# A gated mix of attention and a Mish layer: first scores by halves of the tokens, head group 0 first, Mish in six 16-bit instructions, and a newly planned order

## The chip, the cores and the metric

The kernel runs on one core of a Trainium2 chip. The core's engines take their own instructions in their own order and wait for each other by semaphores: TensorE (PE, matmuls into PSUM; its weight loads are listed as PEld), VectorE (DVE), ScalarE (ACT), GpSimd (POOL) and SyncE (SP, which here only starts transfers). The metric is the device time of one execution in microseconds, the median of several runs.

## The reference

For 2048 tokens x of 640 numbers in bfloat16, two layers are computed and mixed by a gate of each token:

```python
x = A_x
g = _sigmoid((x * gate_w).sum(-1, keepdims=True))
a = _A_ref(x, A_wqkv, A_wo)       # attention: 32 heads of 20, all 2048 keys, softmax, @ wo
b = _B_ref(x, B_w1, B_b1, B_w2)   # h = x @ w1 + b1 (1536 wide); h * tanh(softplus(h)); @ w2
return g * a + (1 - g) * b
```

The attention's scale is 20 ** -0.5. The largest part is 32 heads x 2048 x 2048 scores, each with an exponential.

## The kernel before, in words

**Tiling.** The tokens are cut into four chunks of 512 (index c, as queries), the heads into eight groups of four (index g). A group's four heads lie in rows 32 apart, 20 rows used and 12 zero, so that four score matmuls of 32 rows run side by side in the array. For a pair (c, g) there are 16 key tiles of 128 (kt) and four heads (j): 64 *units*, each one bank of 128 keys x 512 queries; 2048 units in all. The last pair is split into two halves of 256 queries (`CUTS`).

**A unit's way.** PE computes its scores (line 1206, from QT and KT). Then one of two engines takes the exponential. ScalarE takes two or three units in one instruction (line 1233, "ETS", a pair of 1024 elements or a triple of 1536 per partition) out of one of two sets of three PSUM banks. Or VectorE takes a unit alone ("block", line 1291): it turns the scaled score into an integer whose bits are a 16-bit float near the exponential; when a tile's four heads are done, two shading passes (line 1321, 128x2048 int16) make two shifted copies, and the three are weighed with copies of V that GpSimd scales (line 1346, "VS"). PE multiplies all with V (line 1442) into one accumulator bank (ACC); V has a column of ones in front, so a row of the result is the softmax's sum.

**A pair's end.** VectorE copies the accumulator (line 1533, "OUNG"); three transfers on SP's queue and a reciprocal spread the inverted sums (RR, SUMS, BCT), and GpSimd multiplies (line 1499) into QT, which now holds the attention's output. For the last halves VectorE does this alone (lines 1518 to 1526).

**The start.** SP loads the first 512 tokens as rows in two halves (slots `xr0`, `xr1`), then the other chunks by transposing loads (`xt1`, `xt2`), three loads of the remaining query, key and value weights, and the last chunk (`xt3`). ScalarE loads its table and then issues group 0's weights (`wq0`, `wk0`, `wv0`). PE turns the rows by matmuls with a unit matrix (line 787); the query and key weights of group 0 are copied by GpSimd into zeroed areas with 32 columns a head (PADQ, PADK, line 599) and projected (lines 796 and 775). Keys and queries of the other groups are projected in rows of 128 or 120, written to memory and fetched back in the padded layout. PE fills waits with matmuls that nothing reads (line 1732; ten ahead of the start, line 576).

**The other layer.** h is computed for 256 tokens at a time (`h_task`, 48 evictions, line 984), and for two evictions at once Mish (`mish`): ScalarE takes tanh (line 1008), VectorE three instructions of 1024 float32 elements (lines 1025 to 1027). There are 24 Mish. The second product (`b_task`), the output product of the attention (`p_task`, `part_task`) and the mix with the gate (line 1064) follow; the last chunk's come at the very end.

**What sets the order.** The whole program is laid out on the host by a planner, and each engine executes its list as it stands. `Plan.add` keeps a clock for each engine with fixed costs (`EXP_PAIR`, `WIDE`, `BROAD`, `TAIL`). Per step one ScalarE exponential is placed; ahead of it come the scores of two steps later, with a third unit or a block for VectorE as the rules allow; between them PE gets the value products and the tasks (projections and the other layer), sorted by due times in steps; VectorE's queue of small work (`blend` for Mish, `soon` for shading) is filled into the gaps that the planner sees. The thresholds of these rules are constants which the table `STRETCHES` replaces from given steps on:

```python
if fast and step in STRETCHES:
    globals().update({**USUAL, **STRETCHES[step]})
```

The pairs' sequence is `groups`: for each g the chunks 0 and 1, and after all g the chunks 2 and 3 with all their groups. A second program for scores beyond a bound stands behind a flag and does not run.

Of the kernel before, what the change touches and what calls it, by code (L numbers as in the profile page):

```python
# [17 lines left out]
P = 128  # L18
S = 2048
D = 640  # L20
# [74 lines left out]
BROAD = 1.13  # L95
# [13 lines left out]
CALM = 10  # L109
# [5 lines left out]
H_AT = 160  # L115
H_STEP = 13.632
# [17 lines left out]
    11: {"BUSY": 0.327, "LATER": 0.616, "LOAD": 0.63, "MARGIN": 1.659, "OVER": 0.315, "PATIENCE": 7.796, "VMIN": 2.077},  # L134
    33: {"BEHIND": 29.477, "BUSY": 0.327, "FREE": 0.045, "KEPT": 12, "LATER": 0.616, "LOAD": 0.63, "MARGIN": 1.659, "NEED": 3, "OVER": 0.315, "PATIENCE": 7.796, "VMIN": 2.077},
    55: {"AHEAD": 49, "BEHIND": 29.477, "BUSY": 0.516, "CROWD": 1.326, "EAGER": 161, "FMIN": 0.057, "FREE": 0.045, "KEPT": 11, "LATER": 0.616, "LOAD": 0.63, "MARGIN": 1.659, "NEED": 3, "OVER": 0.284, "PATIENCE": 7.796, "ROOM": 2.074, "SLACK": 0.21, "THIRD": 0.53, "VMIN": 2.077, "XSLACK": 0.452},
    77: {"AHEAD": 49, "BEHIND": 29.477, "BUSY": 0.516, "CALLED": 8.459, "CROWD": 1.326, "EAGER": 161, "FMIN": 0.057, "FREE": 0.045, "KEPT": 12, "LATER": 0.616, "LOAD": 0.63, "MARGIN": 1.659, "NEED": 3, "OVER": 0.284, "PATIENCE": 13.174, "ROOM": 2.074, "SLACK": 0.21, "THIRD": 0.53, "VMIN": 2.077, "XSLACK": 0.452},
    97: {"MARGIN": -0.33, "ROOM": 1.622, "VMIN": 1.002},
    119: {"BUSY": 1.408, "EAGER": 125, "FREE": 0.15, "LOAD": 0.572, "MARGIN": -0.33, "NEED": 2, "OVER": 0.193, "ROOM": 1.622, "VMIN": 1.002},
    141: {"LATER": 0.556, "LOAD": 0.574, "MARGIN": 2.071, "OVER": 0.124, "SPUN": 0.577, "STREAM": 0.516, "XLATE": 6.941},  # L140
    163: {"AHEAD": 29, "CROWD": 1.874, "EAGER": 48, "FMIN": 0.467, "MARGIN": 0.792, "PATIENCE": 6.502, "SLACK": 0.282, "VMIN": 0.963},
    185: {"FREE": 0.148, "MARGIN": 1.463, "THIRD": 0.244, "XSLACK": 0.494},
    206: {"AHEAD": 45, "KEPT": 6, "THIRD": 0.693},
    227: {"BUSY": 0.518, "MARGIN": 1.193, "SPARED": 2},
# [142 lines left out]
def bass_gated_mix__softmax_full_mha__dense_activation_mish__prompt_kernel(  # L287
# [123 lines left out]
    def attention(pl, fast):  # L411
# [1580 lines left out]
```

## Time and profile before

| | |
|---|---|
| runs, us | 763.28, 759.77, 760.76; median 760.76 |
| the profiled execution | 761.41 us; its span from first to last instruction 759.6 us |
| busy: PE, DVE, ACT, POOL | 731.4, 697.2, 737.7, 200.3 us |
| granted TensorE clock | 0.998 |
| ScalarE exponentials | 703 pairs, 46 triples |
| VectorE blocks, shading passes | 504, 252 |
| first exponential starts, last ends | 10.15, 750.94 us |

An engine's busy time is the union of its instructions, and the mean duration of one overlaps the next a little, so the price of one in a dense row is better read from a stretch. Idle time in square brackets stands ahead of a row, with what ended it.

### The profile page before, as it was taken

What the parts mean: (1) busy time and instruction counts of PE and PEld (TensorE: products, weight loads), DVE (VectorE), ACT (ScalarE), POOL (GpSimd) and SP (SyncE); (2) the same over time, 40 slices, a digit from 0 to 9 for tenths busy, and PEclk for the clock granted to TensorE, in tenths of its full rate; (3) what the DMA queues carried; (4) which work ended last, traced back from release to release, by engine and by line L of the source; (5) the groups of instructions that cost most, each with busy time, mean ns of one, the idle gap of its engine ahead of it and who ended that gap; (6) DMA issues with size and microseconds to landing.
All of it is one profiled execution on the core that took longest, in us unless ns stands there. A gap on an engine that the chain in (4) does not pass through costs nothing.

```text
span 759.6 us, 25333 instructions
## 1 busy us (share of the span) xinstructions
PE 731.4 (96%) x11227; PEld 275.0 (36%) x11232; DVE 697.2 (92%) x1124; ACT 737.7 (97%) x780; POOL 200.3 (26%) x305
## 2 busy tenths in 40 slices
PE   8999999999999999889999999999999999998996
PEld 3333344334333433223333334333443433342343
DVE  3599878999999999997899999999999999999896
ACT  5999999999999999999999999999999999999995
POOL 3212233203223311342121333112442032322222
PEclk9999999999999999999999999999999999999999
DMA  9422421122134122361232122201212211300001
GB/s 222 75 67 50 120 66 35 59 66 58 50 105 116 47 81 68 98 177 43 53 61 67 37 68 68 78 11 54 84 51 63 83 29 38 90 26 16 16 7 51
DMA packets 78012, 50.41 MB, mean 66 GB/s; under 512 B 21408, under 2 KB 73880, under 8 KB 77848
## 3 DMA queue, kind: packets, MB, share of 16 engines
q1 hardware_dynamic: 75528, 48.24, 23.5%
q8 instruction: 90, 1.47, 0.8%
q10 hardware_dynamic: 2256, 0.47, 0.3%
q0 software_dynamic: 112, 0.01, 0.2%
q14 instruction: 26, 0.21, 0.1%
HBM read 39.01 MB, written 8.90 MB: 63 GB/s over the span
## 4 chain that ended last, share of the span: by engine, by line
PE 37%; ACT 32%; DVE 23%; DMA 4%; SPq 1%; issue 1%; POOL 1%; ACTq 0%; DVEq 0%
ACT ETS L1233 31%; PE PS L1206 12%; PE PS L507 12%; PE PS L1442 10%; DVE LN L1291 7%; DVE LN L1321 5%; DVE REG L1291 2%; PE PS L850 2%; DMA XB<-in_A_x_dram 2%; DMA BCT<-SUMS 1%; DVE U L1026 1%; SPq L556 1%; DVE HB L1027 1%; ACT REG L1008 1%; DVE HB L984 1%
## 5 line engine op out<-in xcount | busy, mean ns | idle before, releaser
L1233 ACT ACTIVATE ETS<-PS 128x1024 bf16<-128x1024 f32 (+1 forms) x749 | 716.0, 1117 | 7.1 <-PE PS L1206 6.0
L1206 PE MATMUL PS<-QT,KT 32*128 32x512 bf16 (+1 forms) x2120 | 293.5, 378 | 11.0 <-ACT ETS L1233 9.1
L1291 DVE TENSOR_SCALAR LN<-PS 128x512 int16<-128x512 f32 x400 | 266.5, 680 | 16.8 <-PE PS L1206 15.5
L1499 POOL TENSOR_TENSOR QT<-OUNG,BCT 128x512 bf16<-128x512 f32 x31 | 43.7, 1411 | 471.6 <-DMA BCT<-SUMS 471.6
L1346 POOL TENSOR_SCALAR VS<-V_all 128x84 bf16<-128x84 bf16 x260 | 149.1, 574 | 65.9 <-DVE V_all L831 26.3
L1206 PEld LDWEIGHTS PS<-QT,KT 32*128 32x128 bf16 x2120 | 73.0, 91 | 237.5 <-ACT ETS L1233 198.0
L1442 PE MATMUL PS<-ETS,V_all 128*21 128x512 bf16 (+1 forms) x1592 | 148.4, 376 | 0.4 <-DVE V_all L831 0.3
L1321 DVE TENSOR_SCALAR LN<-LN 128x2048 int16<-128x2048 int16 x178 | 126.7, 714 | 5.7 <-PE PS L1442 5.4
L507 PE MATMUL PS<-XB,REG 128*32 128x256 bf16 (+2 forms) x1860 | 95.8, 299 | 1.5 <-DMA XB<-in_A_x_dram 0.8
L1442 PE MATMUL PS<-LN,VS 128*21 128x512 f16 (+1 forms) x804 | 76.5, 379 | 2.9 <-DVE LN L1321 2.8
L507 PE MATMUL PS<-W2R,HB 128*32 128x320 bf16 x1536 | 75.4, 301 | 0.6 <-DVE LN L1291 0.4
L1442 PEld LDWEIGHTS PS<-ETS,V_all 128*21 128x21 bf16 x1592 | 37.9, 90 | 56.2 <-issue 45.7
L507 PEld LDWEIGHTS PS<-XB,REG 128*32 128x32 bf16 x1860 | 42.4, 95 | 30.7 <-issue 20.7
L507 PE MATMUL PS<-WOQ,QT 128*32 128x320 bf16 x1024 | 50.5, 301 | 0.5 <-DVE QT L1526 0.5
L507 PEld LDWEIGHTS PS<-W2R,HB 128*32 128x32 bf16 x1536 | 34.6, 96 | 26.9 <-issue 14.0
L1291 DVE TENSOR_SCALAR REG<-PS 128x512 int16<-128x512 f32 x56 | 37.1, 679 | 3.3 <-PE PS L1206 3.3
L1442 PE MATMUL PS<-LN,V_all 128*21 128x512 f16 (+1 forms) x408 | 39.0, 377 | 0.0
L507 PE MATMUL PS<-XB,WOQ 128*32 128x512 bf16 (+2 forms) x440 | 35.1, 382 | 0.8 <-DVE WOQ L739 0.4
L1442 PEld LDWEIGHTS PS<-LN,VS 128*21 128x21 bf16 x804 | 19.1, 89 | 42.3 <-issue 21.5
L984 DVE TENSOR_TENSOR HB<-PS,B1F 128x512 bf16<-128x512 f32 x48 | 32.5, 677 | 0.1
L507 PEld LDWEIGHTS PS<-WOQ,QT 128*32 128x32 bf16 x1024 | 23.4, 96 | 17.2 <-issue 8.0
L850 PE MATMUL PS<-REG,XB 128*128 128x160 bf16 (+1 forms) x240 | 24.5, 234 | 0.4 <-DVE V_all L860 0.2
(118 smaller groups left out, 502.1 us busy)
## 6 DMA issues: line engine op xcount, KB each, us to landing
REG<-in_B_w_dram SPq DMA_DIRECT2D x36, 320.0 KB, 3.3
BCT<-SUMS SPq DMA_DIRECT2D x31, 256.0 KB
W2R<-in_B_w_dram SPq DMA_DIRECT2D x12, 320.0 KB, 5.6
QT<-QS SPq DMA_DIRECT2D x28, 128.0 KB, 2.8
KT<-KS SPq DMA_DIRECT2D x28, 128.0 KB
KS<-LN SPq DMA_DIRECT2D x16, 128.0 KB, 4.0
QS<-WOQ SPq DMA_DIRECT2D x16, 120.0 KB
W2R<-in_B_w_dram SPq DMA_DIRECT2D x12, 160.0 KB, 5.2
```

The source lines that it names most:

```text
L507: last = e.matmul(to[at + j:at + j + n, :], w[:, j:j + n], x, start=start, stop=stop, tile_position=(0, at + j))
L556: "sp", lambda e: e.dma_start_transpose(xt(c), x_ap[c * CW:(c + 1) * CW, :]), (), f"xt{c}", cost=4.5)]
L850: return lambda e, bank: e.matmul(PS[:, bank, i * n:(i + 1) * n], xt(t // 4)[:, f, t % 4 * P:(t % 4 + 1) * P], WV[:, f, g * HD:g * HD + n] ...
L984: ev = dve(lambda e: e.tensor_tensor(hb, PS[:, bank, :].rearrange("p (i t) -> p i t", i=2), bias, ALU.add), [last, *b1f, *guarded, *b_read ...
L1008: ex = pl.add("act", lambda e: e.activation(U, h, AF.Tanh, bias=BEND, scale=0.5), [ev, u_free[0]], cost=0.94)
L1206: op = pl.add("pe", lambda e, to=to, g=real(g), tile=tile, j=j, cols=cols, c=c, of_q=of_q: e.matmul(to[:, cols], KT[32 * j:32 * j + 32, g, ...
L1233: e_op[s] = pl.add("act", lambda e: e.activation(RING[:, p:p + n, :], scores(s)[:, 0:n, :], AF.Exp, scale=SCALE), [s_op[s], *(pv_slot[b] f ...
L1291: bank_free[bank] = x_ops[bank] = tile["op"] = dve(lambda e: e.tensor_scalar(dst, PS[:, bank, :], SCALE * ULPS, BASE, ALU.mult, ALU.add), ...
L1321: op = pl.add("dve", lambda e: e.tensor_scalar(to, src, SHADES[n] - SHADES[held], None, ALU.add), [made, *deps], cost=SHADE, port=True)
L1346: weighted[(c, g, k)] = n, [pl.add("pool", lambda e, i=i, n=n, src=src: e.tensor_scalar(VS[:, n, i, :, :], src, WEIGHTS[i + 1], None, ALU. ...
L1442: lasts[n] = pl.add("pe", lambda e, v=v, j=j, src=src[:, cols], of_q=of_q, begin=begin, end=end: e.matmul(PS[32 * j:32 * j + EW, ACC, of_q ...
L1499: oung_free[0] = bc_read[0] = otn_done[(c, g)] = pl.add("pool", lambda e: e.tensor_tensor(otn(c, g), src, BC, ALU.mult), deps, cost=TIMES, ...
```

## The change

The first scores: the ten transposes of the first 256 tokens, their queries and their keys come ahead of all work on the second 256. Queries (chunk 0) and keys (all chunks) of group 0 are projected straight from the loaded weights, 20 columns a head, by the new `heads`; PADK is gone, PADQ stays for the other chunks' queries. The scores of the first two key tiles are cut into halves of the queries. ScalarE issues group 0's weight loads ahead of its table load; six matmuls, not ten, stand ahead of the start; the accumulator's fill moves behind the first keys.

The order: `groups` starts with group 0 of all four chunks, then groups 1 to 7 of chunks 0 and 1 in turn, then chunk 2, then chunk 3. Some planner costs and due times are new (loads' tails, `K_AT`, `V_AT`, `CALM` 10 to 6), and the whole `STRETCHES` table is.

Mish: the same polynomial of tanh, factored, on two halves of U2 seen as float16, with a factor `LIFT` that the gate's constant takes out again. U is free after the first of the six.

```diff
-BROAD = 1.13
+FULL = 0.60
+SCALED = 0.34
+LIFT = 512.0
...
-    11: {"BUSY": 0.327, "LATER": 0.616, "LOAD": 0.63, "MARGIN": 1.659, "OVER": 0.315, "PATIENCE": 7.796, "VMIN": 2.077},
...
+    119: {},
+    141: {"LOAD": 0.475, "OVER": 0.255},
...
-            groups = [(c, g) for g in range(NG) for c in range(2)] + [(c, g) for c in range(2, NC) for g in range(NG)]
+            groups = [(c, 0) for c in range(NC)]
+            groups += [(c, g) for cs in ((0, 1), (2,), (3,)) for g in range(1, NG) for c in cs]
...
+            if fast and (c, g) == (0, 0) and kt < 2:
+                return [(i, slice(i * HW, (i + 1) * HW), slice(kt * HW, (kt + 1) * HW)) for i in range(2)]
...
+            wload("wq0", WQ[:, :, 0:HD], wqkv[:, :, 0:HD], 4.4)
+            wload("wk0", WK[:, :, 0:HD], wqkv[:, :, D:D + HD], 4.4)
+            wload("wv0", WV[:, :, 0:HD], wqkv[:, :, 2 * D:2 * D + HD], 7.3)
             pl.add("act", lambda e: e.activation(U2[:, 0:1], RING[:, 0, 0:1], AF.Exp), [m_zero], cost=1.5)
-            wload("wq0", WQ[:, :, 0:HD], wqkv[:, :, 0:HD])
-            wload("wk0", WK[:, :, 0:HD], wqkv[:, :, D:D + HD])
-            wload("wv0", WV[:, :, 0:HD], wqkv[:, :, 2 * D:2 * D + HD])
...
-            for i in range(10):
+            for i in range(6):
...
+            def heads(e, to, w, x, start, stop):
+
+                for j in range(HG):
+                    last = e.matmul(to[32 * j:32 * j + DH, :], w[:, DH * j:DH * j + DH], x, start=start, stop=stop, tile_position=(0, 32 * j))
+                return last
...
+                bank_free[0] = turn(0, [0, 1], 0, "dve")
+                bank_free[1] = turn(0, [2, 3], 1, "act")
+                bank_free[3] = turn(0, [4], 3, "dve")
                 q, k = QT[:, 0, 0:CW], KT[:, 0, 0:CW]
...
+                last = project(5, WQ, lows, w_load["wq0"], lows, 0)
+                first = copy("dve", q[:, lows], PS[:, 5, lows], last, 0.34)
+                q_done.update({(0, 0, j): [first] for j in range(HG)})
+                last = project(FB, WK, lows, w_load["wk0"], lows, 0)
+                k_done[(0, 0)] = copy("act", k[:, lows], PS[:, FB, lows], last, 0.34)
+                bank_free[2] = turn(1, [0, 1], 2, "dve")
+                high = turn(1, [2], 5, "act", 1, [first])
+                acc_free[0] = turn(1, [3, 4], ACC, "dve")
...
-                G = U2[:, :]
+                A, B = (U2[:, n * CW:(n + 1) * CW].bitcast(F16) for n in range(2))
...
-                piece(BROAD, lambda e: e.scalar_tensor_tensor(U, U, a, U, ALU.add, ALU.mult))
-                piece(BROAD, lambda e: e.scalar_tensor_tensor(G, U, b, h, ALU.add, ALU.mult))
-                piece(BROAD, lambda e: e.scalar_tensor_tensor(h, U, c, G, ALU.add, ALU.mult), done)
+                piece(FULL, lambda e: e.tensor_scalar(A, U, LIFT, LIFT, ALU.mult, ALU.add), taken)
+                piece(SCALED, lambda e: e.tensor_scalar(B, A, 1 / LIFT, a - 2, ALU.mult, ALU.add))
+                piece(FULL, lambda e: e.tensor_tensor(A, A, B, ALU.mult))
+                piece(SCALED, lambda e: e.tensor_scalar(B, A, 1 / LIFT, b - c, ALU.mult, ALU.add))
+                piece(FULL, lambda e: e.tensor_tensor(A, A, B, ALU.mult))
+                piece(FULL, lambda e: e.tensor_tensor(h, A, h, ALU.mult), done)
```

Counted over the lists of the engines, ScalarE's exponentials are now 651 pairs, 79 triples and one single; VectorE has 508 blocks and 254 shading passes; the 24 tanh stay. The last 18 of these stand between the 380th and the 695th of 749 exponentials before, and between the 357th and the 619th of 731 now.

The start on PE, before (LN holds the token rows, ETS the zeros of the warm-up, XB the turned tokens, WOQ and REG the query and key weights):

```order
L576 MATMUL PS<-ETS 128x512 x9
L787 MATMUL PS<-LN 128x128 [waits f_pool,f_xr0]
L787 MATMUL PS<-LN 128x128
L787 MATMUL PS<-LN 128x128 [waits f_xr1]
L787 MATMUL PS<-LN 128x128 x17
L796 MATMUL PS<-XB,WOQ 128x512 [waits f_pool,f_dve]
```

and in the changed kernel:

```order
L580 MATMUL PS<-ETS 128x512 x5
L781 MATMUL PS<-LN 128x128 [waits f_pool,f_xr0]
L781 MATMUL PS<-LN 128x128 x9
L602 MATMUL PS<-XB,WOQ 20x256 [waits f_wq0,f_dve]
L602 MATMUL PS<-XB,WOQ 20x256 x7
L602 MATMUL PS<-XB,WOQ 20x256 [waits f_act]
L602 MATMUL PS<-XB,WOQ 20x256 x7
L602 MATMUL PS<-XB,WOQ 20x256 [waits f_dve]
L602 MATMUL PS<-XB,WOQ 20x256 x3
L602 MATMUL PS<-XB,REG 20x256 [waits f_wk0]
```

The wait for the second half of the rows (`f_xr1`) stood behind two transposes and now stands behind both projections of the first half; the projections wait for the loads themselves, not for GpSimd.

The wait for the fourth chunk (`f_xt3`) on PE, before:

```order
L1206 MATMUL PS<-QT,KT 128x512 [waits f_act]
L1206 MATMUL PS<-QT,KT 128x512
L823 MATMUL PS<-REG,XB 128x80 x12
L1206 MATMUL PS<-QT,KT 128x512 [waits f_act]
L1206 MATMUL PS<-QT,KT 128x512
L823 MATMUL PS<-REG,XB 128x80 x5
L507 MATMUL PS<-XB,REG 32x512 [waits f_xt3]
```

and in the changed kernel:

```order
L1224 MATMUL PS<-QT,KT 128x512 [waits f_act]
L1224 MATMUL PS<-QT,KT 128x512
L1224 MATMUL PS<-QT,KT 128x512 [waits f_dve]
L1224 MATMUL PS<-QT,KT 128x512 [waits f_act]
L1224 MATMUL PS<-QT,KT 128x512
L1224 MATMUL PS<-QT,KT 128x512 [waits f_dve]
L602 MATMUL PS<-XB,REG 20x512 [waits f_dve,f_xt3]
```

Ahead of that wait stood the scores of 14 exponentials and none for VectorE; now those of 17 and five blocks (two are the single scores that wait for `f_dve` here).

A Mish on VectorE, before (REG, W2R and U2 are its work areas, HB holds h):

```order
L1025 SCALAR_TENSOR_TENSOR W2R<-W2R 128x1024
L1291 TENSOR_SCALAR LN<-PS 128x512 [waits f_pe]
L692 CAST LN<-PS 128x512 [waits f_pe]
L1291 TENSOR_SCALAR LN<-PS 128x512 [waits f_pe]
L1533 COPY OUNG<-PS 128x512 [waits f_pool,f_pe]
L1321 TENSOR_SCALAR LN<-LN 128x2048
L739 CAST WOQ<-PS 128x512 [waits f_pe]
L1026 SCALAR_TENSOR_TENSOR U2<-W2R,HB 128x1024
```

and in the changed kernel:

```order
L1038 TENSOR_SCALAR U2<-W2R 128x1024 [waits f_act]
L1039 TENSOR_SCALAR U2<-U2 128x1024 [waits f_dve]
L1309 TENSOR_SCALAR LN<-PS 128x512 [waits f_pe]
L870 CAST V_all<-PS 128x3x8x20 [waits f_pe]
L1040 TENSOR_TENSOR U2<-U2 128x1024 [waits f_dve]
L1041 TENSOR_SCALAR U2<-U2 128x1024 [waits f_dve]
L1309 TENSOR_SCALAR LN<-PS 128x512 [waits f_pe]
L737 CAST WOQ<-PS 128x512 [waits f_pe]
L1309 TENSOR_SCALAR LN<-PS 128x512 [waits f_pe] x2
L1042 TENSOR_TENSOR U2<-U2 128x1024
L1043 TENSOR_TENSOR HB<-U2,HB 128x1024 [waits f_dve]
```

The pieces still stand among blocks and evictions; there are twice as many, and some now follow each other directly. At the very end five mixes (line 1064, now 1080) stand behind VectorE's last division, where there were three.

More of the change, by code (lines that the diff above doesn't have):

```diff
@@ L115 @@
 H_AT = 160
+V_AT = 4
+K_AT = 3
 H_STEP = 13.632
@@ L1551, in attention @@
         if fast:
[L1552 to L1554 removed]
+            more, most = first_keys()
             for s in range(2):
```

251 lines of the change are left out of this document (120 added, 131 removed).

## The prediction

> **What bounds the kernel now.** I read the shares of the page first, then the chain of waits by engine and line, then ScalarE's rows by form and its timeline, and last the waits.
>
> ```profile
> PE 731.4 (96%) x11227; PEld 275.0 (36%) x11232; DVE 697.2 (92%) x1124; ACT 737.7 (97%) x780; POOL 200.3 (26%) x305
> PE 37%; ACT 32%; DVE 23%; DMA 4%; SPq 1%; issue 1%; POOL 1%; ACTq 0%; DVEq 0%
> PEld PS L1206 <- ACT ETS L1233: 198.0, 562, 1.2
> ACT ETS L1233 <- PE PS L1206: 6.0, 13, 1.2
> ```
>
> Three engines are above 90%, and the chain passes through all of them. Who sets the pace is told by the waits: the score matmuls wait 562 times, 198.0 us, for a softmax exponential to give its PSUM banks back, while ScalarE waits only 13 times, 6.0 us, for scores. PE's 96% holds matmuls put in to keep it busy. So the time is: when ScalarE starts, the sum of its instructions, its waits, and what follows its last exponential.
>
> ```profile
> 9.29 0.37 ACT L771 CAST KT<-PS 128x256 bf16<-128x256 f32 x1 [1.62 <-PE PS L775]
> 10.15 1.94 ACT L1233 ACTIVATE ETS<-PS 128x1024 bf16<-128x1024 f32 x2 [0.49 <-PE PS L1206]
> 12.62 11.11 ACT L1233 ACTIVATE ETS<-PS 128x1024 bf16<-128x1024 f32 x12 [0.53 <-PE PS L1206]
> 24.43 86.24 ACT L1233 ACTIVATE ETS<-PS 128x1024 bf16<-128x1024 f32 x91 [0.69 <-PE PS L1206]
> 111.87 75.83 ACT L1233 ACTIVATE ETS<-PS 128x1024 bf16<-128x1024 f32 x82 [1.20 <-PE PS L1206]
> ...
> 188.53 22.14 ACT L1233 ACTIVATE ETS<-PS 128x1024 bf16<-128x1024 f32 x24
> 210.51 1.10 ACT L1008 ACTIVATE W2R<-HB 128x1024 f32<-128x1024 bf16 x1
> ...
> 310.48 70.95 ACT L1233 ACTIVATE ETS<-PS 128x1536 bf16<-128x1536 f32 x70 [0.41 <-PE PS L1206]
> 381.10 1.27 ACT L1008 ACTIVATE REG<-HB 128x1024 f32<-128x1024 bf16 x1
> ...
> 746.32 4.62 ACT L1233 ACTIVATE ETS<-PS 128x1536 bf16<-128x1536 f32 x4 [0.51 <-PE PS L1206]
> ```
>
> ScalarE's first exponential starts at 10.15, its last ends at 750.94; 8.7 us of the span follow. Of its idle time, 10.2 us lie ahead of the first exponential.
>
> **The change, part by part.**
>
> *Exponentials.* The order of the changed kernel has 651 pairs (1024 elements), 79 triples (1536) and one single; before there are:
>
> ```profile
> L1233 ACT ACTIVATE ETS<-PS 128x1024 bf16<-128x1024 f32 x703 | 662.0, 1089 | 6.0 <-PE PS L1206 5.1
> L1233 ACT ACTIVATE ETS<-PS 128x1536 bf16<-128x1536 f32 x46 | 70.7, 1537 | 1.1 <-PE PS L1206 0.9
> L1233 ACT ACTIVATE ETS<-PS 128x1024 bf16<-128x1024 f32 x82 | 75.7, 1122 | 1.4 <-PE PS L1206 1.2
> L1233 ACT ACTIVATE ETS<-PS 128x1024 bf16<-128x1024 f32 x55 | 53.8, 1102 | 0.0
> L1233 ACT ACTIVATE ETS<-PS 128x1536 bf16<-128x1536 f32 x15 | 23.1, 1540 | 0.4 <-PE PS L1206 0.4
> ```
>
> The first two rows are of the whole run, the third of 111.87 to 187.59, the last two of 310.48 to 381.10. Mean durations overlap, so prices come from stretches: 82 pairs in 75.7 us is 0.923 each; 55 pairs and 15 triples fill 70.62 us (381.10 - 310.48), so a triple is (70.62 - 55 x 0.923) / 15 = 1.32. Before: 703 x 0.923 + 46 x 1.32 = 709.6. After: 651 x 0.923 + 79 x 1.32 + 0.52 for the single (an estimate: a pair less the 0.40 between pair and triple) = 705.7. That is -3.9. Part of 0.923 is small waits; the 21.98 us from 188.53 to the tanh at 210.51 hold 24 pairs, 0.916 each, which makes the triple 1.35 and the saving -2.6. I take -3.2. The 24 tanh (L1008) stay.
>
> *The start.* The chain to the first exponential:
>
> ```profile
> 0.73 1.28 ACT L564 ACT_TABLE_LOAD   x1 [0.73 <-PEq L1977]
> 0.74 0.96 SPq L550 DMA_DIRECT2D LN<-in_A_x_dram  x2
> 1.17 0.49 ACTq L544 DMA_DIRECT2D WOQ<-in_A_wqkv_dram  x1
> 1.19 4.45 PE L576 MATMUL PS<-ETS 128*128 128x512 bf16 x10 [1.19 <-DVE ETS L562]
> 6.06 1.18 PE L787 MATMUL PS<-LN 128*128 128x128 bf16 x18 [0.21 <-DMA LN<-in_A_x_dram]
> 6.16 0.52 POOL L599 COPY WOQ<-WOQ 128x400 bf16<-128x400 bf16 x1 [4.69 <-DMA WOQ<-in_A_wqkv_dram]
> 6.94 0.52 POOL L599 COPY REG<-REG 128x400 bf16<-128x400 bf16 x1 [0.27 <-DMA REG<-in_A_wqkv_dram]
> 8.55 0.71 PE L775 MATMUL PS<-XB,REG 128*128 128x256 bf16 x5
> 8.75 0.69 DVE L772 CAST QT<-PS 128x512 bf16<-128x512 f32 x1 [0.48 <-PE PS L796]
> 23.66 0.40 PE L507 MATMUL PS<-XB,REG 128*32 128x512 bf16 x4 [0.82 <-DMA XB<-in_A_x_dram]
> LN<-in_A_x_dram SPq DMA_DIRECT2D x2, 320.0 KB, 4.1
> ```
>
> Query weights land just before 6.16, key weights just before 6.94. The changed kernel issues them ahead of the table load instead of behind it, at about 0.75 where it was 1.17, so 0.4 us earlier: near 5.7 and 6.5. The three issues, some 0.5 us each, push the table load back to about 3.7, still ahead of ScalarE's first copy. The token rows come by two loads, issued at 0.74 and 1.25, that land 4.1 us behind their issues in the middle; the second ends PE's wait at 6.06, 4.8 behind its issue, so the first takes 3.4 and is there at 4.1. Its ten transposes and three copies (0.69 and less, on two engines) are done before the weights come. Then, by the rows here: query projection 0.7, from 5.8 to 6.5; key projection 0.7, from 6.6 to 7.3; key copy 0.4, to 7.7; the six transposes of the second half stand ahead of the scores, to 8.0; scores to the first exponential 0.45 (9.66 to 10.15 before): 8.5, with the padding copies (L599) gone from the chain. The removed fills and copies on VectorE and GpSimd cost nothing: they lay in the wait for the loads.
>
> What that is worth is set by another landing. The matmuls that wait for the fourth token block (23.66) stand in PE's order behind the scores of 14 exponentials before, of 17 after; SP's queue up to that load is unchanged, so it lands at the same time. 17 x 0.923 from 8.5 is 24.2, and the next scores come 23.66 + 0.6 (twelve matmuls) + 0.45 = 24.7. So the eighteenth exponential starts near 24.7; before it would be 24.43 + 3 x 0.923 = 27.2. The head gives -2.5. If the start slips to 9.5, the eighteenth starts at 25.2 and the head gives -2.0; if the weights land no earlier and copies queue, to 10.15, -1.4. The lower end is -2.6, since the fourth block's landing caps it.
>
> The warm-up is six matmuls, not ten; at 0.43 us for 512 columns they run at half the pace of L775 (0.71 us for five of 256, of which some 0.27 is the last one's latency). If the array is still slow at 5.8, both projections take about 0.5 us more each and the start is 9.5, the case above. The Trainium skill, page "TensorE: Matmul & The Clock Gate", Part 1, says that the first 3.4 us or so of activity run at half clock and that an idle window brings that back; by it six matmuls (2.6 us) and a gap would make this slow start the likely one, 0.5 us of the time.
>
> *Mish.* Three 1024-element instructions in float32 become six in 16 bits.
>
> ```profile
> L1291 DVE TENSOR_SCALAR LN<-PS 128x512 int16<-128x512 f32 x400 | 266.5, 680 | 16.8 <-PE PS L1206 15.5
> L1321 DVE TENSOR_SCALAR LN<-LN 128x2048 int16<-128x2048 int16 x178 | 126.7, 714 | 5.7 <-PE PS L1442 5.4
> L1025 DVE SCALAR_TENSOR_TENSOR REG<-REG 128x1024 f32<-128x1024 f32 x18 | 21.9, 1214 | 0.3 <-ACT REG L1008 0.3
> 443.01 1.20 DVE LN L1291 x2
> 457.85 1.13 DVE HB L1027
> 370.00:690.00 320.00, 311.64 (x482) 1.00 0.21 56
> ```
>
> The pieces of the chain show 0.60 for what lasts 0.680 and 1.13 for what lasts 1.21, so 0.08 of each overlaps: before, 3 x 1.13 = 3.40. No row has the new forms. Their ends: all at L1321's rate (2048 in 0.60, so 1024 in about 0.33), 2.0; the four with two sources or a float32 source at L1025's 1.13, 5.2. I take half of L1321's rate for those four, because they are 16-bit and move twice its bytes per element: 4 x 0.60 + 2 x 0.33 = 3.07. That frees 0.33 x 24 = 7.9 us of VectorE; four more score blocks and two more shading passes (0.60 each) take 3.6 of it. None of it is in the sum: the order is fixed, and VectorE's work sits behind ScalarE's. If the cover goes, it costs what the second rival says. The page "VectorE: DVE Perf Modes" of the Trainium skill speaks against the change in "Rules for kernel authors": it wants few instructions, and its fixed 150 cycles or so each would leave 3.6 for the six against 3.67 for the three, 1.6 us of VectorE in all; no run here shows the new forms yet.
>
> *Group 0 first.* Queries and keys of the other groups are due later, and VectorE gets score blocks early: five stand ahead of the fourth block's wait, where before it did 5.30 us of work in 20:
>
> ```profile
> 10.00:30.00 20.00, 17.82 (x237) 7.30 (x233) 5.30 (x11) 18.62 (x21) 6.49 (x14) 1.00 0.81 180
> ```
>
> Those blocks are four units fewer for ScalarE, counted above. The division's transfers move ahead of the first query and key writes on SP; their next reader is three groups off. Nothing added.
>
> *The end.*
>
> ```profile
> 751.43 0.45 DVE L1520 STREAM_TRANSPOSE U<-PS 128x256 f32<-128x256 f32 x1 [0.25 <-PE PS L1442]
> 753.62 1.47 DVE L1064 SCALAR_TENSOR_TENSOR HB<-PS,GATE,W2R 128x320 bf16<-128x320 f32 x3 [0.56 <-PE PS L507]
> ```
>
> Behind the last division stood three mixes, now five, each 0.49. The two new ones fill most of the 0.56 that VectorE waits for PE: +0.4, between 0 and +1.0.
>
> **The sum.** The profiled execution took 761.41 (span 759.6 and 1.8 around it). -3.2 - 2.5 + 0.4 = -5.3, with ScalarE's other waits (4.3 of the 6.0 us) as before: 756.1. The runs shown have their median 0.65 lower, 760.76, so 755.5 against that.
>
> **Rivals.** *More waits.* The order was laid out with fixed costs, and ScalarE meets each misfit as a wait. For it: the waits at 111.87 (1.20) and 746.32 (0.51) are such misfits, and 54 triples' banks more are shared with VectorE's blocks; 18 of 24 Mish now stand closer together. Against: the same layout left only 13 waits. If the 4.3 us double and the start is slow, 756.1 - 0.65 + 4.3 + 0.5 = 760.3, no measurable change; from three times on nothing is left.
>
> *VectorE becomes the bound where Mish lies.* From 370 to 690 it is busy 311.64 of 320 us, 8.4 idle. If the four doubtful pieces take 1.13 each, Mish is 5.2, 1.8 more than before; 24 times that is 43 us, and with the 3.6 us of added blocks, less the 8.4, VectorE ends 38 us late. ScalarE's saving is then worth nothing, and only head and end count: 760.8 - 2.5 + 0.4 + 38 = 797. If only the three pieces with two sources take 1.13, Mish is 3 x 1.13 + 0.60 + 0.67 = 4.66, and the same sum gives 784. It is slower than before by 0.5% (764.6) when Mish takes 0.45 us more than before, 3.85 in all, which is 0.80 for each of the four pieces. Against: the 16-bit row from SBUF (L1321) passes four elements where L1025 passes one, and 0.80 lies nearer to 1.13 than to that.
>
> *Waits go.* The freed 4.3 us of VectorE (7.9 - 3.6) bring blocks earlier, ScalarE's remaining 4.3 us of waits vanish: 751.2.
>
> **How the numbers follow.** Forecast 0.50, waits go 0.14, more waits 0.25, VectorE bound 0.11. The forecast's own range, from its terms (exponentials 1.3, head 1.1, end 0.6 on the far side), is 753.5 to 758. Taking in both neighbours gives 750.5 to 763, with the VectorE case left out. A measurement of this kernel tells about 0.5% from no change: 757.0 and 764.6 are the bounds. Faster takes the waits-go case and most of the forecast, 0.60; same the more-waits case and the forecast's rest, 0.29; slower 0.11.
>
> **What would show it.** First exponential near 8.5; the eighteenth near 24.7; a wait for the fourth block at 23.6; ScalarE's exponentials in 705 us instead of 709; two-source Mish pieces of about 0.68 mean, one-source of about 0.42; ScalarE's waits for scores around 5 us; the last exponential ending near 745. Mish rows of 1.2, ScalarE waiting over 12 us for scores, or a first exponential behind 9.5 would make it wrong.

## The result, and the profile after

The changed kernel takes 756.36 us (median of five runs, 755.65 to 757.22) where the kernel before takes 760.55 (759.16 to 763.28): a ratio of 0.995, 95% interval 0.9932 to 0.9968. The profiled execution took 756.36 us, its span 754.6 instead of 759.6.

The page after, busy shares and chain by engine; then two rows of the waits (us, times, longest) and ScalarE's exponentials by form (busy, mean ns | idle ahead of them):

```profile
PE 725.5 (96%) x11326; PEld 275.6 (37%) x11326; DVE 695.8 (92%) x1203; ACT 734.1 (97%) x762; POOL 186.2 (25%) x306
PE 39%; ACT 34%; DVE 20%; DMA 3%; SPq 1%; issue 1%; POOL 1%; ACTq 0%; DVEq 0%
```

```profile
PEld PS L1224 <- ACT ETS L1251: 203.9, 570, 1.1
ACT ETS L1251 <- PE PS L1224: 4.9, 13, 0.9
```

```profile
L1251 ACT ACTIVATE ETS<-PS 128x1024 bf16<-128x1024 f32 x651 | 621.5, 1097 | 4.6 <-PE PS L1224 3.6 <-PE PS L1461 0.2
L1251 ACT ACTIVATE ETS<-PS 128x1536 bf16<-128x1536 f32 x79 | 123.2, 1563 | 1.3 <-PE PS L1224 1.3
```

The picture is the one of before: three engines above 90%, the chain through all of them, and again 13 waits of ScalarE for scores, 4.9 us where it was 6.0. ScalarE's timeline of the head, after:

```profile
8.09 1.94 ACT L1251 ACTIVATE ETS<-PS 128x1024 bf16<-128x1024 f32 x2 [0.18 <-PE PS L1224]
16.07 8.80 ACT L1251 ACTIVATE ETS<-PS 128x1024 bf16<-128x1024 f32 x9 [0.17 <-PE PS L1461]
25.32 6.03 ACT L1251 ACTIVATE ETS<-PS 128x1024 bf16<-128x1024 f32 x6 [0.46 <-PE PS L1224]
32.27 3.28 ACT L1251 ACTIVATE ETS<-PS 128x1536 bf16<-128x1536 f32 x3 [0.92 <-PE PS L1224]
```

The 5.05 us of the span lie so: the first exponential starts 2.06 us earlier (8.09, 10.15 before), first start to last end takes 4.27 less (736.52, 740.79 before), and behind the last exponential the tail is 1.29 longer (9.95, 8.66 before). VectorE's Mish, by form:

```profile
L1038 DVE TENSOR_SCALAR U<-REG 128x1024 f16<-128x1024 f32 x18 | 12.8, 710 | 0.0
L1039 DVE TENSOR_SCALAR U<-U 128x1024 f16<-128x1024 f16 x24 | 10.1, 422 | 0.3
L1040 DVE TENSOR_TENSOR U<-U 128x1024 f16<-128x1024 f16 x24 | 17.1, 712 | 0.1
L1043 DVE TENSOR_TENSOR HB<-U,HB 128x1024 bf16<-128x1024 f16 x24 | 16.3, 680 | 0.1
```

### The profile page after: what moved, and what is told of

It reads as the page before. It is cut to its first block, busy times and chain, and to the rows that moved or that the text cites. A ratio compares the mean times of both kernels' runs of the same rounds, so it can differ in the third digit from the quotient of the medians.

```text
span 754.6 us, 25638 instructions
## 1 busy us (share of the span) xinstructions
PE 725.5 (96%) x11326; PEld 275.6 (37%) x11326; DVE 695.8 (92%) x1203; ACT 734.1 (97%) x762; POOL 186.2 (25%) x306
## 4 chain that ended last, share of the span: by engine, by line
PE 39%; ACT 34%; DVE 20%; DMA 3%; SPq 1%; issue 1%; POOL 1%; ACTq 0%; DVEq 0%
ACT ETS L1251 32%; PE PS L1224 13%; PE PS L1461 12%; PE PS L513 10%; DVE LN L1309 7%; DVE LN L1339 4%; PE PS L860 2%; DMA XB<-in_A_x_dram 2%; DVE HB L994 1%; SPq L562 1%; ACT REG L1018 1%; DMA QS<-WOQ 1%; PE PS L901 1%; DVE U L1038 1%; DMA BCT<-SUMS 1%
## 5 line engine op out<-in xcount | busy, mean ns | idle before, releaser
L1224 PE MATMUL PS<-QT,KT 32*128 32x512 bf16 (+1 forms) x2139 | 289.1, 377 | 13.3 <-ACT ETS L1251 10.1
L1224 PEld LDWEIGHTS PS<-QT,KT 32*128 32x128 bf16 x2139 | 72.5, 91 | 237.0 <-ACT ETS L1251 203.9
L1364 POOL TENSOR_SCALAR VS<-V_all 128x84 bf16<-128x84 bf16 x262 | 135.6, 518 | 47.0 <-DVE LN L690 16.8
L1339 DVE TENSOR_SCALAR LN<-LN 128x2048 int16<-128x2048 int16 x183 | 130.6, 719 | 5.8 <-PE PS L1461 5.2
L513 PE MATMUL PS<-XB,REG 128*32 128x256 bf16 (+2 forms) x1800 | 87.5, 295 | 0.7 <-DVE XB L1057 0.4
L1309 DVE TENSOR_SCALAR REG<-PS 128x512 int16<-128x512 f32 x60 | 40.3, 681 | 2.8 <-PE PS L1224 2.7
```

What stands on the lines that cost most here:

```text
L513: last = e.matmul(to[at + j:at + j + n, :], w[:, j:j + n], x, start=start, stop=stop, tile_position=(0, at + j))
L1224: op = pl.add("pe", lambda e, to=to, g=real(g), tile=tile, j=j, cols=cols, c=c, of_q=of_q: e.matmul(to[:, cols], KT[32 * j:32 * j + 32, g, ...
L1309: bank_free[bank] = x_ops[bank] = tile["op"] = dve(lambda e: e.tensor_scalar(dst, PS[:, bank, :], SCALE * ULPS, BASE, ALU.mult, ALU.add), ...
L1339: op = pl.add("dve", lambda e: e.tensor_scalar(to, src, SHADES[n] - SHADES[held], None, ALU.add), [made, *deps], cost=SHADE, port=True)
L1364: weighted[(c, g, k)] = n, [pl.add("pool", lambda e, i=i, n=n, src=src: e.tensor_scalar(VS[:, n, i, :, :], src, WEIGHTS[i + 1], None, ALU. ...
```

## The experiments

All keep each engine's list as it stands but for the edit named. A ratio is to the kernel before, run beside it on the same chip; medians of before were 760.57, 760.62 and 761.47 us in the three groups of four experiments, each group on a chip of its own. The changed kernel's ratio, 0.995, is from its own group with a median of 760.55, so a difference between runs of two groups is given by the ratios, or by both.

### Mish and VectorE

**Mish alone, in the order of before.** Three slots became six instructions, the extra ones one VectorE instruction away from the slots.

```diff
-                piece(BROAD, lambda e: e.scalar_tensor_tensor(U, U, a, U, ALU.add, ALU.mult))
...
+                piece(BROAD, six[0], three.append)
+                piece(BROAD, six[2], three.append)
+                piece(BROAD, six[5], lambda op: (three.append(op), done(op)))
...
+            op = Op("dve", six[n], [first], None)
+            ops.insert(at + (ops[at] not in three), op)
```

> The kernel before in its own order on every engine; only Mish is the six 16-bit instructions, two of them (about 0.93 us together) around each slot where one float32 instruction (1.13 us) stood. Forecast's theory (ScalarE sets the pace, VectorE's work is covered): no change, 759.5 to 761.3, the 703 pairs and 46 triples as before, ScalarE's waits for scores near 6 us. Rival (the relief of VectorE, 8 us, carries the gain of the change): 753 to 757.

Measured 763.59 us, ratio 1.0034 (1.0011 to 1.0058): slower than either expected. In the old order six instructions cost 2 to 3 us more than three, although VectorE has less to do. What of it could be found is shown below.

**The relief taken back, once and four times over.**

```diff
+        for _ in range(times):
+            last = Op("dve", fn, [last], None)
...
+            ops.insert(at, last)
...
+    again(fast.ops, 1)
```

> The changed kernel in its own order, with one of Mish's one-source instructions (0.33 us) done a second time, in all 24 Mish: +8 us on VectorE, as much as the 16-bit form freed. Theory: VectorE is idle 8.5 us from 370 to 690, where 18 of the Mish lie, so 756.4 to 758.4. Rival (VectorE at its limit, the freed time is needed): 762 to 765.

> As the last, but the one-source instruction done four more times: +32 us on VectorE, 24 of them from 370 to 690. Theory, by the rule of the forecast's second rival: VectorE is the bound there, 24 less its 8.5 idle, +15.5: 768 to 776. If VectorE is far from setting the pace: under 760. If it sets the pace all along: 784 to 790.

Measured 763.5 (ratio 1.0028, 1.0007 to 1.005) and 802.64 (1.0552, 1.0518 to 1.0585). In the first the repeated instruction takes 0.33 us from its start to the next, 8 us in all, and the kernel loses 5.9 us against the changed one (1.0028 - 0.995 of 760.6; 7.1 by the medians). In the second the repeats wait for one another, 0.43 us of busy time each, 41 us in all, and it loses 46, more than any of the three expectations. ScalarE's waits for scores, of the first and of the second:

```profile
ACT ETS L1252 <- PE PS L1225: 8.1, 18, 1.0
```

```profile
ACT ETS L1252 <- PE PS L1225: 38.3, 58, 2.0
```

So the rival holds: most of VectorE's added 8 us is paid, although the changed kernel's trace shows 8.5 us of it idle from 370 to 690. With a Mish as long as it was, the new order is slower than the kernel before (1.0028).

The 46 us of the second are not VectorE's time alone. PE has more pauses there, and in eight stretches of 3.4 us between 382 and 693 the clock granted to TensorE is 0.50. Two of them (us, then busy time of PE, PEld, DVE, ACT, POOL; the clock is the third number from the end):

```profile
382.20:385.50 3.30, 3.30 (x28) 0.62 (x26) 2.34 (x4) 2.05 (x2) 1.26 (x3) 0.50 0.87 92
399.20:402.50 3.30, 3.30 (x47) 1.65 (x46) 2.65 (x5) 2.89 (x3) 0.00 (x0) 0.50 0.03 3
```

The eight stretches, each with the pause ahead of it, hold 23 of the 47 us by which the last exponential ends later than in the changed kernel's trace; pause and clock were not taken apart. The trace of the first run has no such stretch before the program's end.

**Half of Mish's work left out on VectorE, then of ScalarE's tanh too.**

```diff
+                A, B, U, hh = A[:, 0:CW], B[:, 0:CW], V[:, 0:CW], h[:, 0:CW]
...
-                piece(FULL, lambda e: e.tensor_tensor(h, A, h, ALU.mult), done)
+                piece(FULL, lambda e: e.tensor_tensor(hh, A, hh, ALU.mult), done)
```

```diff
-                ex = pl.add("act", lambda e: e.activation(V, h, AF.Tanh, bias=BEND, scale=0.5),
+                ex = pl.add("act", lambda e: e.activation(V[:, 0:CW], h[:, 0:CW], AF.Tanh, bias=BEND, scale=0.5),
```

> The changed kernel in its own order, with Mish's six instructions over half of their elements only (the other half of the hidden layer goes on without Mish, so this leaves out part of the computation): about 34 us less on VectorE, ScalarE as it was. Theory: ScalarE's sum stays, at most its waits in the Mish stretch go: 753.5 to 756.5. Rival (VectorE sets the pace together with ScalarE): 745 to 751.

> The changed kernel with Mish's six instructions and its tanh over half of the elements (part of the computation is left out): as the run with half of Mish's VectorE work, and ScalarE has 24 x about 0.42 = 10 us less besides (a tanh takes 0.95 for 1024 elements; half of one is estimated at 0.53). Theory (ScalarE sets the pace where VectorE is relieved): 744 to 747. Rival (VectorE, or the order between the engines, would hold it up all the same): 750 to 754.

Measured 754.8 (0.9915, 0.9893 to 0.9936) and 754.55 (0.9929, 0.9903 to 0.9954). From start to start the half instructions take 0.33 to 0.45 and 0.21 to 0.23 us instead of 0.60 and 0.33, which is 25 us less on VectorE and not the 34 expected; they give about 2 us (1.6 to 2.7 by ratios and medians). The half tanh takes 0.52 instead of 0.95, 10 us less on ScalarE, and that gives nothing more. Here the theory falls: ScalarE's sum does not come through. The stretch from 370 to 690 (us, then busy time of PE, PEld, DVE, ACT, POOL), of the changed kernel and of the one with both halves left out:

```profile
370.00:690.00 320.00, 312.98 (x5435) 123.76 (x5431) 311.49 (x536) 318.02 (x331) 81.38 (x124) 1.00 0.20 54
```

```profile
370.00:690.00 320.00, 313.51 (x5461) 123.89 (x5453) 297.66 (x538) 314.58 (x333) 78.35 (x124) 1.00 0.20 54
```

VectorE has room now, and the program keeps its length. The busy times alone do not tell who holds it: ScalarE, 314.6 of 320 us, is as near to its limit as PE, 313.5. The waits and the chain point to PE. ScalarE's waits for scores, 5.2 us with half of VectorE's Mish left out, are longer when its own work is cut, and PE's share of the chain is 58%, 39% in the changed kernel:

```profile
ACT ETS L1252 <- PE PS L1225: 8.9, 24, 2.0
PE 58%; ACT 30%; DVE 6%; DMA 4%; SPq 1%; issue 0%; DVEq 0%
```

The waits of 198.0 us (203.9 in the changed kernel) that I had read as PE's are those of weight loads, and PE went on with other matmuls meanwhile. PE itself was idle ahead of score matmuls for 11.0 us in the kernel before and 13.3 in the changed one:

```profile
L1206 PE MATMUL PS<-QT,KT 32*128 32x512 bf16 (+1 forms) x2120 | 293.5, 378 | 11.0 <-ACT ETS L1233 9.1
```

```profile
L1224 PE MATMUL PS<-QT,KT 32*128 32x512 bf16 (+1 forms) x2139 | 289.1, 377 | 13.3 <-ACT ETS L1251 10.1
```

### GpSimd's multiplication

Behind the head ScalarE has nine waits over 0.15 us in the changed kernel. Seven of them, 2.2 of 3.1 us, stand within 3 us behind one thing; the longest, 0.74 us at 304.8, does not. The timeline around one of the seven (start, duration, engine, line; weight loads and some rows left out):

```profile
630.03 1.69 POOL L1521 TENSOR_TENSOR QT<-OUNG,BCT 128x512 bf16<-128x512 f32 x1 [16.41 <-DMA BCT<-SUMS]
...
630.50 1.77 DVE L1339 TENSOR_SCALAR LN<-LN 128x2048 int16<-128x2048 int16 x1
...
632.20 0.68 DVE L1309 TENSOR_SCALAR LN<-PS 128x512 int16<-128x512 f32 x1
...
632.93 0.46 PE L513 MATMUL PS<-W2R,HB 128*32 128x320 bf16 x8 [1.12 <-DVE LN L1309]
633.31 0.39 PE L1224 MATMUL PS<-QT,KT 32*128 32x512 bf16 x2
...
633.74 1.02 ACT L1251 ACTIVATE ETS<-PS 128x1024 bf16<-128x1024 f32 x1 [0.28 <-PE PS L1224]
```

A shading pass that takes 0.68 us lasts 1.77: it ends 0.55 us behind GpSimd's multiplication of a finished group, which ends at 631.72. The block behind the pass is late, PE waits 1.12 us for the bank that it holds, the scores stand behind that on PE, and ScalarE waits. Counted over the trace, VectorE instructions of 1024 or 2048 elements that last over 0.15 us beyond their median: 14 in the changed kernel, 9.3 us in all; 12 in the kernel before, 8.8 us. Each of them overlaps such a multiplication, and all 14 end 0.55 us behind it. Four of the 12 are float32 instructions of the old Mish, so 16 bits are no condition; no instruction that reads PSUM is late by as much. The Trainium skill, page "SBUF — State Buffer", section "SBUF: two separate sides", has this rule: VectorE and GpSimd share one pair of ports, held exclusively for a whole instruction, and "the other fully blocks". The rows agree: 1.77 us for 0.68.

```diff
-                oung_free[0] = bc_read[0] = otn_done[(c, g)] = pl.add("pool", lambda e: e.tensor_tensor(
-                    otn(c, g), src, BC, ALU.mult), deps, cost=TIMES, port=True)
+                def parts(e):
+                    for n in range(4):
+                        cut = slice(n * CW // 4, (n + 1) * CW // 4)
+                        last = e.tensor_tensor(otn(c, g)[:, cut], src[:, cut], BC[:, cut], ALU.mult)
+                    return last
```

> The changed kernel with GpSimd's multiplication of a finished group by its inverse sums (1.27 us, 31 times) issued as four instructions of 128 columns. In the trace, 14 of VectorE's 16-bit instructions from its own memory last until such a multiplication has ended, 9.3 us in all, and most of ScalarE's waits over 0.2 us stand behind them. Theory (the multiplication shuts VectorE out while it runs): in shorter pieces each wait is 0.3 us at most, 3 us in all or less, and 3 to 5 of ScalarE's 9 us of such waits go: 751.5 to 753.5. Rival (what keeps VectorE is not the one instruction's length): 756 to 757.

Measured 752.86 us, ratio 0.9908 (0.9883 to 0.9933), 3.2 us under the changed kernel by the ratios, 3.5 by the medians. The late instructions are 8 now, 1.9 us in all. The shading passes (min/median/max ns) of the changed kernel and of this one, and this one's chain and ScalarE's waits:

```profile
L1339 DVE TENSOR_SCALAR LN<-LN x183: 674/683/1773, 26.0 to 743.4; 128x2048 int16<-128x2048 int16 x183
```

```profile
L1339 DVE TENSOR_SCALAR LN<-LN x183: 675/683/947, 26.9 to 739.6; 128x2048 int16<-128x2048 int16 x183
```

```profile
ACT 43%; PE 39%; DVE 12%; DMA 3%; POOL 1%; issue 1%; ACTq 0%; DVEq 0%
```

```profile
ACT ETS L1251 <- PE PS L1224: 1.8, 4, 0.9
```

The longest pass is 0.95 us instead of 1.77, ScalarE's waits fall from 4.9 to 1.8 us, the seven waits named above are gone, and VectorE's share of the chain from 20% to 12%: the theory holds, with its time.

**The same in the kernel before, and with Mish alone in it.** The edit is the one above; the second adds the first experiment's.

```diff
+                        last = e.tensor_tensor(otn(c, g)[:, cut], src[:, cut], BC[:, cut], ALU.mult)
...
+                piece(BROAD, six[0], three.append)
```

> The kernel before in its own order, with GpSimd's multiplication of a finished group in four instructions of 128 columns, as in the last run of the changed kernel. In the trace of before 12 of VectorE's instructions, 8.8 us in all, last until such a multiplication ends. Theory (both kernels pay this price, so it is no part of what the change gave): 756.5 to 758.5. Rival (it costs only the new order): 760 to 761.

> As the last, and Mish in six 16-bit instructions around its old slots. Theory (Mish alone cost 2.6 us because more of its instructions, and the shadings behind them, fell on a multiplication of GpSimd): as the last within 1 us. Rival (score blocks pushed back by up to 0.6 us in an order laid out for three instructions): 1.5 to 3 us over the last. Second rival (the freed 8 us of VectorE are worth something by themselves): 2 us or more under it.

Measured 756.78 (0.9936, 0.991 to 0.9961) and 760.67 (0.9996, 0.9972 to 1.0021). The first: both kernels pay this price alike, so it is no part of the change; one edit of GpSimd gives the kernel before as much as the whole change did. The second: with the multiplication in four Mish alone still costs 3.9 us by the medians, more than without that edit, so its loss was not the multiplication's, and the first rival holds. In the two traces the last exponential starts 3.3 us later; 0.8 of that arises at 25 us, where scores wait for the fourth token block, long before the first Mish at 187, and the other 2.5 lie within the rival's 1.5 to 3. Its largest step, 1.0 us, in the timeline of that run:

```profile
607.04 0.89 DVE L1031 TENSOR_TENSOR HB<-U,HB 128x1024 bf16<-128x1024 f16 x1
...
607.85 1.27 DVE L1300 TENSOR_SCALAR LN<-PS 128x512 int16<-128x512 f32 x2
...
608.58 0.86 PE L508 MATMUL PS<-W2R,HB 128*32 128x320 bf16 x20 [0.24 <-DVE LN L1300]
...
610.29 0.40 PE L1451 MATMUL PS<-LN,VS 128*21 128x512 f16 x4 [0.20 <-DVE LN L1330]
...
612.00 1.94 ACT L1242 ACTIVATE ETS<-PS 128x1024 bf16<-128x1024 f32 x2 [0.93 <-PE PS L1215]
```

Two blocks stand behind Mish's last instruction, PE waits for their bank and for the shading behind them, and ScalarE waits 0.93 us. VectorE has less to do in all, but at this place it is late. The four parts of a multiplication run there as well, from 605.05 to 607.38, and make up a part of it: the last two instructions of Mish take 0.83 and 0.89 us instead of 0.68.

**Both halves left out, with the multiplication in four.** The edits of two runs above together.

```diff
+                A, B, U, hh = A[:, 0:CW], B[:, 0:CW], V[:, 0:CW], h[:, 0:CW]
...
+                        last = e.tensor_tensor(otn(c, g)[:, cut], src[:, cut], BC[:, cut], ALU.mult)
```

> The changed kernel with GpSimd's multiplication in four, and Mish's instructions and its tanh over half of the elements (part of the computation is left out): VectorE has 34 us less, ScalarE 10 us less than in the run with the multiplication in four alone (752.9). Theory (TensorE, 98% busy from 370 to 690, sets the pace there as well): 750 to 753. Rival (ScalarE alone sets it): 742 to 745.

Measured 751.39 us, ratio 0.9861 (0.9826 to 0.9896). With 25 us of VectorE and 10 of ScalarE away, 1.5 us are gained over 752.86 by the medians, 3.6 by the ratios. From 370 to 690, of the run with the multiplication in four and of this one:

```profile
370.00:690.00 320.00, 314.68 (x5464) 123.98 (x5455) 310.60 (x542) 319.90 (x335) 90.56 (x166) 1.00 0.20 54
```

```profile
370.00:690.00 320.00, 314.82 (x5479) 124.50 (x5475) 295.58 (x543) 316.27 (x336) 84.36 (x166) 1.00 0.20 54
```

In the first ScalarE is at its limit, 319.90 of 320. In the second it is not, and waits longer for scores, 6.9 us where it was 1.8:

```profile
ACT ETS L1252 <- PE PS L1225: 6.9, 14, 1.8
```

This fits ScalarE and PE setting the pace together. That PE, 314.8 busy in both, holds the time once ScalarE is relieved is argued from the waits and the chain: no run took matmuls off PE or changed its order.

### Start and tail

**The fourth token block ahead of the large weights.**

```diff
+    x = next(op for op in ops if op.slot == "xt3")
+    ops.remove(x)
+    ops.insert(next(i for i, op in enumerate(ops) if op.slot == "wk"), x)
```

> The changed kernel with SP's load of the fourth token block ahead of the three large weight loads instead of behind them; nothing else is moved. Theory (the fourth block's landing caps the start): it lands near 18 instead of 24.1, PE's wait of 0.89 us at 24.13 goes, the eighteenth exponential starts near 24.6 instead of 25.3, and 0.4 to 0.8 us are left of it at the end: 755.6 to 756.1. Rival: the large weights, now behind it, are late for the queries and values of group 1 near 28 to 31, and ScalarE waits there for over 1 us more: 757 or more.

Measured 757.02 us, ratio 0.9956 (0.9937 to 0.9975): not told apart from the changed kernel by time. The head shows it (ScalarE's timeline of this run):

```profile
16.06 14.40 ACT L1251 ACTIVATE ETS<-PS 128x1024 bf16<-128x1024 f32 x15 [0.17 <-PE PS L1461]
31.39 4.20 ACT L1251 ACTIVATE ETS<-PS 128x1536 bf16<-128x1536 f32 x4 [0.93 <-PE PS L1224]
```

The wait at 25.32 is gone. The eighteenth exponential, inside the first row, starts at 24.75 (25.32 in the changed kernel), the twenty-fourth at 31.39 (32.27), and no new wait stands near 28 to 31. So the fourth block was a cap, of 0.6 to 0.9 us; the rival falls by the trace, though the time lies in its range (twelve runs from 753.32 to 758.73). A wait of 0.93 stays: ahead of the twenty-fourth's scores PE has the first query projection from the large weights, 1.25 us, at 29.77 here and at 30.65 in the changed kernel.

**Three last mixes off VectorE.**

```diff
+        ev.eng = ev.key = "act"
+        ev.fn = lambda e, bank=bank, tb=tb, tmp=tmp, PS=PS, GATE=GATE: e.activation(
+            tmp, PS[:, bank, 0:HALF], AF.Identity, scale=GATE[:, tb:tb + 1])
...
+        got = was[i % 2] = Op("pool", lambda e, dst=dst, tmp=tmp, add=add: e.tensor_tensor(dst, tmp, add, ALU.add), [ev, part], None)
```

> The changed kernel with three of the four last mixes of the first half of the tokens (one ahead of the last division on VectorE, two behind it) done by ScalarE and GpSimd, which are idle there from 744.6 on, as one mix is already; the two instructions take 0.53 and 0.86 us. Theory (the mixes behind the division make the tail longer): the time from the last exponential to the end of the span goes from 9.95 us to 8.8 to 9.3: 755.2 to 755.8. Rival (the tail is set by the output transfers' issue and landing): 9.7 to 10.1, no change.

Measured 757.32 us, ratio 0.9957 (0.9934 to 0.9979); the tail is 10.04 us. The tail is as long as its rival said, but the edit was flawed: one of the three mixes took a buffer that the last division releases, and another stood behind it on ScalarE, so neither could start before the division's end. Only the mix ahead of the division tells something: without it the division ends 2.29 us behind the last exponential instead of 2.50.

**Together.** The multiplication in four, the fourth block, the twenty-fourth's scores ahead of that projection, two more warm-up matmuls and the mixes with free buffers.

```diff
+    spread(fast.ops, (1, 2, 3))
+    sooner(fast.ops)
+    warmer(fast.ops)
+    ahead(fast.ops)
```

> The changed kernel with the multiplication in four, the fourth token block loaded ahead of the large weights, seven warm-up matmuls instead of six and one more behind the first ten transposes (so that TensorE does not pause), the scores of the twenty-fourth exponential ahead of the first query projection from the large weights instead of behind it, and three of the last mixes on ScalarE and GpSimd without the wait for the last division. Estimates from the runs so far: 752.9 less 0.6 for the block, 0.5 to 0.9 for the scores, 0.3 to 0.8 for the tail and up to 0.9 where TensorE started at half pace: 749.5 to 751.5, first exponential at 8.1 to 9. Rival (the start's gain is eaten by later waits, the tail is set by the transfers): 752 to 753.

Measured 751.64 us (750.1 to 755.69 in five runs), ratio 0.9854 (0.9819 to 0.9889): under both kernels, a little above its forecast, and 1.2 us under the multiplication in four alone by the medians, with intervals that overlap. The profiled execution was its slowest, 755.69. In it PE waits 1.80 us for weights from memory; ScalarE loses 2.0 us by that against the changed kernel's trace, and 2.9 more up to 271, with the granted clock at 0.50 until 269 (the second row, as above):

```profile
260.66 0.62 PE L513 MATMUL PS<-XB,W2R 128*32 128x256 bf16 x16 [1.80 <-DMA W2R<-in_B_w_dram]
262.30:269.00 6.70, 6.70 (x56) 2.85 (x53) 4.37 (x10) 4.85 (x6) 3.25 (x7) 0.50 0.47 137
```

The head is as wanted (first exponential 8.39, twenty-fourth 30.66). Of the tail, worked out from the traces, us from each mark to the next:

| | last exponential to the division's end | to the last mix | to the end of the last issue | to the span's end |
|---|---|---|---|---|
| before | 2.11 | 2.03 | 1.02 | 3.50 |
| changed | 2.50 | 2.29 | 1.42 | 3.73 |
| multiplication in four | 2.50 | 2.29 | 0.79 | 4.29 |
| relief taken back | 2.50 | 2.29 | 0.71 | 3.44 |
| together | 2.29 | 2.03 | 1.40 | 4.46 |

The first two columns follow the order of the instructions; the last two, issue and landing of the output, run from 4.15 to 5.86 us together, and from 4.15 to 5.15 in the three rows with one and the same list of the tail. What the mixes gave (0.47 us) lies under that.

## Why the prediction was right, and where its reasons were not

The time (755.5 forecast, 756.36 measured) was right. The sum got there in part by luck: the head and the end gave less than forecast, other waits more, and the errors cancel.

**Exponentials, -3.2 (-2.6 to -3.9).** The counts are as forecast, 651, 79 and one. By the distance from start to start where nothing waits (0.904 us a pair, 1.331 a triple in both traces) the 52 pairs less and 33 triples more are worth -3.1; the single, 0.79 us at the end of the row, takes some 0.6 back, so -2.5, at the near end. No run took this part alone.

**The start, -2.5 (-1.4 to -2.6): mis-sized.** The first exponential came at 8.09, better than 8.5, and the eighteenth at 25.32 (24.7 forecast; 27.17 before), -1.85; the fourth block ended PE's wait at 24.13, not at 23.66 as before. Six pairs later, with only pairs up to there in both kernels, the lead is gone: the twenty-fourth starts at 32.27, 32.67 before, -0.4. Even that is more than the other traces show: over the eight with this start and the fourth block in its old place the twenty-fourth starts at 32.83 in the mean (32.27 to 33.23), over the four with the old start at 32.84 (32.54 to 33.27). The step that failed is "The head gives -2.5": it looked for the next cap at the fourth block alone. That cap is there, and the projection at 30.65 is the next one. The row of the relief taken back shows the same from the other side, a start 1.76 us later that costs 0.8 by the twenty-fourth (ScalarE's timeline of that run):

```profile
9.85 22.28 ACT L1252 ACTIVATE ETS<-PS 128x1024 bf16<-128x1024 f32 x23 [0.60 <-PE PS L1225]
33.05 2.37 ACT L1252 ACTIVATE ETS<-PS 128x1536 bf16<-128x1536 f32 x2 [0.93 <-PE PS L1225]
```

**Other waits, "as before": mis-sized the other way.** From the twenty-fourth exponential to the end of the last, 718.27 us became 712.34, -5.93. The counts explain 2.5 (as above) to 3.9 (the forecast's far end) of it; the other 2.0 to 3.4 us are waits that went, as in the third rival. Of these the trace shows 1.7 us: ScalarE's idle stretches over 0.15 us come to 5.3 us there before and to 3.7 in the changed kernel. The rest would be in shorter ones, which is not shown. Which part of the new order did away with them was not taken apart.

**Mish, "None of it is in the sum": the pieces right, the reason wrong.** The pieces take 0.71, 0.42, 0.71, 0.42, 0.68 and 0.68 (0.68 and 0.42 forecast); the six at 0.60 and 0.33 from start to start make 3.07 as forecast, and the 3.6 estimated with the fixed 150 cycles or so of the Trainium skill's page "VectorE: DVE Perf Modes" (section "Rules for kernel authors" for the rule) does not show. But "VectorE's work sits behind ScalarE's" does not hold: 8 us put back cost 5.9. That the new order already spends what Mish freed would explain why the sum stood without it; no run laid the order out again with the old Mish. The second rival's point, slower by 0.5% from 0.45 us a Mish more than before, counted the 8.4 us of idle time as cover; in the runs, a Mish as long as before already makes the kernel 0.8% slower than the changed one. This idle time, spread over waits for PE, was no cover.

**The bound, "the sum of its instructions" on ScalarE: half right.** That 198 us of weight loads' waits mean that PE has time was the wrong reading; the idle time ahead of PE's own score matmuls, 11.0 us, was the row to read. In a fixed order 10 us off ScalarE gave nothing and 25 off VectorE about 2; a new order, with fewer pairs, more triples and fewer waits, gained.

**The end, +0.4 (0 to +1.0): +1.29.** The instructions make +0.65, +0.39 up to the division's end (overlooked; 0.21 of it is one mix that stands ahead of the division on VectorE) and +0.26 behind it; the other 0.64 is the output's issue and landing, which vary by more than that between runs.

## What to carry to other kernels

Where a planner has filled three engines above 90%, idle time on a timeline need not be cover: test an engine in both directions, a dose more and a dose less, before calling it hidden or the bound. An edit that relieves one engine may give little, or cost, as long as the order is not laid out again for it. And before costing an edit, look for instructions that last longer than their median: here 9 us of them had one cause, and a split of one GpSimd instruction gave the kernel before as much as the whole change.

## What the runs showed of the hardware

**Shared ports.** GpSimd's 128x512 multiplication of two float32 sources (1.28 us in the median) holds up VectorE's instructions from SBUF to SBUF, 16-bit and float32 alike, until it has ended, 1.09 us at most beyond their own time in the two kernels; in four instructions of 128 columns 0.33 at most in the five runs that have them.

**The granted clock behind a pause.** In the last run PE stands still for 1.80 us up to 260.66, and from 262.2 to 269.0 the granted clock is 0.50. With the relief taken back four times over, eight stretches of 3.4 us at 0.50 begin 0.3 to 2.7 us behind pauses of PE of 0.97 to 1.90 us; four other pauses of 1.26 to 2.27 us have none behind them. So a pause can cost more than its own length.

**The array's pace at the start.** Six warm-up matmuls of 512 columns run at 0.43 us each, and what follows differs between runs whose lists start alike. In the changed kernel's trace it is at full pace:

```profile
4.46 0.73 PE L781 MATMUL PS<-LN 128*128 128x128 bf16 x10 [0.53 <-DMA LN<-in_A_x_dram]
5.64 0.72 PE L602 MATMUL PS<-XB,WOQ 128*20 128x256 bf16 x20 [0.45 <-DVE XB L770]
```

and with the relief taken back at half pace until 9.7:

```profile
4.37 1.25 PE L781 MATMUL PS<-LN 128*128 128x128 bf16 x10 [0.44 <-DMA LN<-in_A_x_dram]
5.77 1.25 PE L602 MATMUL PS<-XB,WOQ 128*20 128x256 bf16 x20
```

Of nine traces with this start four show full pace (first exponential 8.1 to 8.3) and five half (9.8 to 9.95), which was the 9.5 case of the forecast. The Trainium skill, page "TensorE: Matmul & The Clock Gate", Part 1, says that the activity window of about 3.4 us runs freely and that the point of change varies from run to run; the traces agree. The two extra matmuls of the last run leave no pause over 0.15 us there; its array changed pace at about 6 us, and one trace does not tell whether they did it.
